# A planned start-up of an attention and mixer kernel: other load paces, phi's maxima on TensorE, another shape for the loads of one weight

## The chip, the cores and the metric

One core of one Trainium2 chip. The metric is the device time of one execution in microseconds (us).

## What is computed

`q`, `k`, `v` are (8 batches, 8 heads, 576 rows, 64) and `phi` (8, 8, 576, 32), all float32; the four mixer weights come as float64.

```python
a = softmax over s of phi                     # per (b, h, m)
k_m = einsum('bhsm,bhsd->bhmd', a, k);  v_m = the same of v
attn = softmax(q @ k_m.T / 8) @ v_m           # 32 memory slots
x = attn, heads side by side                  # (8, 576, 512)
u = x + (relu(x.T @ w_tok1) @ w_tok2).T       # mixes the 576 rows
out = u + relu(u @ w_ch1) @ w_ch2             # mixes the 512 channels, 1536 hidden
```

## The kernel before, in words

The work has two halves. The attention part runs per *quad*: four heads of one batch, so (b, Q) with Q = 0, 1 gives 16 quads. The channel part runs over nine *chunks* of 512 output rows, each in twelve blocks f of 128 hidden units: a first product (`mm_1`, L140, 12 matmuls of 512 columns), a relu that splits its result into a high (ScalarE, L113) and a low part (VectorE, L116), and a second product (`ch2`, `second`, L179, 12 matmuls). Every operand of a product is split in two parts, hence three matmuls for each.

The float64 weights are loaded as pairs of 32-bit words and turned into a high and a low part on the chip (`Piece`): `low_bits` (ScalarE, L615), `join` (VectorE, L620), `signs` (ScalarE, L626), `rebase` (VectorE, L629), `apply` (VectorE, L635), then for each weight in the piece `part_high` (ScalarE, L642) and `part_low` (GpSimd, L646). Piece f holds `w_ch1`'s columns and `w_ch2`'s rows of block f: the tiles `c1h`/`c1l` and, in the profile, `c`. `PartC1.load` (L717) loads `w_ch1`'s 512 rows x 128 columns of float64 by four DMAs; each fills 32 partitions with four rows of 1 KB. `PartC2.load` (L743) is one DMA of 128 rows.

A quad does: load phi, k, v, q; the maximum of phi over the rows; subtract, exponentiate (L312, L322); the product with k and v (`kvp`, L930 in `EarlyQuad`, L345 in `Quad`); scaling; the scores (L975, L413), a softmax over 32 slots; transposes (L987, L952); the token products `Ap` (L519), `Rp` (L538) and four `u` (L559). For batch 0 the maximum across partitions is taken by TensorE: `phi_turn` transposes (L911), `phi_diag` reduces and spreads it on a diagonal (L915), `phi_spread` multiplies it by ones (L921). For batch 1 it is `partition_all_reduce` on GpSimd (L1062), for quad (2,0) likewise, and there its sum too (L1291). `EarlyQuad` gets the sum as a column of ones in the kv product.

The order of the start is not written by hand. Steps for batches 0 and 1, the conversion of all weights, the 23 products of chunk 0, and the first loads of quad (2,0) are `Step`s with an engine, a cost in us, predecessors and `Room`s (buffers that it takes or uses). `plan` (a list scheduler) picks the engine that can begin first, among its steps that can begin within PATIENCE the one with the longest way to the end, and so writes one order for each engine, which then runs in that order. A load's landing is estimated from kb: 270 units per us, where a weight piece counts its words (1024) and 1.5 us of latency is assumed; a GpSimd reduction counts as 8.0 us. Twelve raw buffers ("homes") hold the pieces: `wide` (five buffers shared with activations, two of them for raw pieces, one after piece 7), `st0`, `st1`, and `kv`. Filler matmuls (L877) stand in long planned gaps of TensorE before the first product. From block 12 on a hand-written loop over chunks runs, with attention steps at set places.

SyncE (SP) issues all loads in the planned order; a DMA whose buffer is still in use holds those behind it.

Of the kernel before, what the change touches and what calls it, by code (L numbers as in the profile page):

```python
# [19 lines left out]
P = 128  # L20
# [7 lines left out]
def kernel(  # L28
# [559 lines left out]
    class Piece:  # L588
# [11 lines left out]
        def load(s, room):  # L600
            tag = room.tag
            name = f"raw{s.parts[0].name}"
            if tag == "wide":
                at = wide(I32, name).rearrange("p a (n t) -> p (a n) t", t=2)
            else:
                at = sb.tile([P, 1024, 2], I32, tag=tag, name=name, bufs=1)
# [77 lines left out]
    class PartW2:  # L684
        words, loads = NT * HALF, 2
# [20 lines left out]
    class PartC1:  # L706
        words, loads = DM, 4
# [20 lines left out]
    class PartC2:  # L728
        words, loads = DM, 1
# [39 lines left out]
    class Step:  # L769


        def __init__(s, eng, us, fn, after, take, use, kb):
            s.eng, s.us, s.fn, s.after, s.take, s.kb = eng, us, fn, list(after), take, kb
# [7 lines left out]
    def step(eng, us, fn, *after, take=(), use=(), kb=0):  # L781
        steps.append(Step(eng, us, fn, after, list(take), list(use), kb))
        return steps[-1]
# [3 lines left out]
    def plan():  # L787
# [6 lines left out]
        order, seen = [], set()  # L794
        for z in steps:
            stack = [(z, iter(then[z]))] if z not in seen else []
            seen.add(z)
            while stack:
                y, it = stack[-1]
                for x in it:  # L800
                    if x not in seen:
                        seen.add(x)
                        stack.append((x, iter(then[x])))
                        break
                else:
                    stack.pop()
                    order.append(y)
        for z in order:
            lag = 2.0 + z.kb / 270 if z.eng == "SP" else LAG.get(z.eng, 0.07)
            way[z] = z.us + lag + max((way[x] for x in then[z]), default=0)  # L810
        free, taken, landed = {}, {}, 0.0
        left, done = set(steps), []

        def when(z):
            t = free.get(z.eng, 0.0)
            for y in z.after:
                if y.ready is None:
                    return None
                t = max(t, y.end if y.eng == z.eng != "SP" else y.ready if z.eng != "SP" or y.eng != "SP" else y.end)
# [20 lines left out]
        while left:  # L840
            times = {}
            for z in left:
                t = when(z)
                if t is not None:
                    times[z] = t
            first = {}
            for z, t in times.items():
# [4 lines left out]
                key=lambda z: (way[z], -steps.index(z)),  # L852
# [11 lines left out]
            done.append(z)  # L864
        return sorted(done, key=lambda z: z.begin)

    PATIENCE = 0.3
    LATE = 3
    now = [None]

    def ps_tile(room, shape, name):

        pool = pch if room.tag == "ch" else pat if room.tag == "at" else pacc
        t = pool.tile(shape, F32, tag=room.tag, name=name, bufs=dict(room.tags)[room.tag])
# [9 lines left out]
    class EarlyQuad(Quad):  # L884
# [153 lines left out]
        def loads(s):  # L1038
# [3 lines left out]
            s.l_phi = step("SP", 1.25, s.load_phi, take=[s.phi], kb=288)  # L1042
            s.l_kv = step("SP", 2.5 * len(s.kvs), s.load_kv, take=s.kvs, kb=1152)
            s.l_q = step("SP", 3.1, s.load_q, take=[s.qroom], kb=576)

        def plan(s, w1, w2, taken, chunk):


            s.up = {}

# [7 lines left out]
            if s.b:  # L1058

                def reduce():  # L1060
                    s.r = sb.tile([P, 4 * M], F32, tag="pr", name="prr" + s.n, bufs=3)
                    nc.gpsimd.partition_all_reduce(s.r, s.m, P, RED.max)  # L1062

                z = step("POOL", 8.0, reduce, z, take=[pr2], use=[pr])
                where = pr2
            else:
                bk, where, col = s.bank(), s.bank(), s.of("ps", 2)
                z = step("PE", 0.3, lambda: s.phi_turn(bk), z, take=[bk], use=[pr])
                z = step("DVE", 0.6, s.phi_diag, z, take=[col, pr2], use=[bk])
                z = step("PE", 0.6, lambda: s.phi_spread(where), z, take=[where], use=[pr2])  # L1070

            z = step("DVE", 0.83, s.phi_sub, z, use=[s.phi, where])
            z = step("ACT", 0.76, s.phi_only_exp, z, use=[s.phi])

# [81 lines left out]

    def piece(tags, *parts, after=(), more=()):

        p = Piece(*parts)
        us = 0.12 + 1.08e-3 * p.words  # L1160
# [3 lines left out]
            take=[raw, *more], kb=p.words,  # L1164
        )
        loads.append(z)
        z = step("ACT", us - 0.05, p.low_bits, z, use=[raw])
        z = step("DVE", us, p.join, z, use=[raw])
        y = step("ACT", us, p.signs, z, use=[raw])
        z = step("DVE", 0.15 + 0.54e-3 * p.words, p.rebase, z, use=[raw])  # L1170
        z = step("DVE", us, p.apply, y, z, use=[raw])
        out = []
        for x, part in enumerate(parts):
            us = 0.12 + 1.08e-3 * part.words
            h = step("ACT", us, lambda x=x: p.part_high(x), z, take=part.rooms(), use=[raw])
            pool = True
            l = step(
                "POOL" if pool else "DVE", 0.15 + 2.3e-3 * part.words if pool else us,
                lambda x=x: p.part_low(x, nc.gpsimd if pool else nc.vector), h, use=[raw],
# [7 lines left out]
    WIDE, KV = [("wide", 5)], [("kv", 1)]  # L1187
# [7 lines left out]
    homes = [WIDE, ST[0], ST[1], WIDE, WIDE, ST[0], ST[1], WIDE, WIDE, KV, WIDE, KV]  # L1195
# [42 lines left out]
    def first_product(f):  # L1238
        bk, hh, hl = Room(("ch", 2)), Room(("hh", 2)), Room(("hl", 2))

        def mm():
# [4 lines left out]
            2.76, mm, *w_c[f][0], *(a.lows + c.lows if f == 0 else ()), take=[bk], use=room0  # L1246
# [31 lines left out]
    ends = [  # L1278
        step("SP", 2.5, second.load_kv, *w_c[NF - 1][1], take=[kv2], kb=1152),
        step("SP", 9.0, second.load_q, quads[1, 1].x_A, take=[q2], kb=576),  # L1280
        took2,
    ]
    for op, name in ((RED.max, "prr"), (RED.add, "psr")):
        pr, pr2 = Room(("pr", 3)), Room(("pr", 3))

        def red(op=op):
            second.m = second._red(ALU.max if op == RED.max else ALU.add)

        def reduce(op=op, name=name):
            second.r = sb.tile([P, 4 * M], F32, tag="pr", name=name + second.n, bufs=3)  # L1290
            nc.gpsimd.partition_all_reduce(second.r, second.m, P, op)  # L1291

        z = step("DVE", 1.3, red, z, take=[pr], use=[phi2])
        z = step("POOL", 8.0, reduce, z, take=[pr2], use=[pr])
        if op == RED.max:
            z = step("DVE", 0.83, second.phi_sub, z, use=[phi2, pr2])
            z = step("ACT", 0.76, second.phi_only_exp, z, use=[phi2])
    o0 = Room(("wide", 5))
    for x in range(NKK):
        ends.append(  # L1300
            step(
                "POOL", 1.4, lambda x=x: chunks[0].residual([x]), *a.lows, *c.lows, products[-4],
                use=[*room0] + ([o0] if x else []), take=[] if x else [o0],
            )
        )
# [131 lines left out]
```

## Time and profile before

| | us |
|---|---|
| median of 3 runs | 848.76 (848.4 to 850.31) |
| the profiled execution | 849.89 |
| its span, first to last instruction | 848.1 |
| TensorE matmul busy | 805.1 (95%) |
| VectorE busy | 411.7 (49%) |
| ScalarE busy | 221.6 (26%) |
| GpSimd busy | 139.6 (16%) |

The mean granted TensorE clock is 0.978 of full. PE is TensorE's matmuls, PEld its weight loads, DVE VectorE, ACT ScalarE, POOL GpSimd, SPq the DMA queue of SyncE. Spans on POOL are rough for library operations: the record of a reduction is a mark within the time that it holds the engine. In a timeline "x4" merges four instructions, and the bracket gives the idle time before the row and what ended it.

### The profile page before, as it was taken

Reading aid. Unit: us, or ns where it says so; the run is one execution under the profiler, and the core shown is the slowest. Engines: PE = TensorE matmul, PEld = TensorE weight load, DVE = VectorE, ACT = ScalarE, POOL = GpSimd, SP = SyncE. Lnnn points to the kernel's source line nnn. Section 1 sums busy time; section 2 is a strip of 40 time slices with the busy share of each in tenths; the row PEclk is TensorE's granted clock in tenths of the full one; section 3 lists DMA queues with packets and bytes.
Section 4 is the critical chain, followed back from the end, with each engine's and each line's share of the span. In section 5 each row is a group of like instructions: output and inputs, shape, how many; then the busy total and the mean of one; then the engine's idle time right before and its main releaser. Section 6 shows DMA issues by size and latency. Waiting matters only on the chain.

```text
span 848.1 us, 11688 instructions
## 1 busy us (share of the span) xinstructions
PE 805.1 (95%) x4648; PEld 660.3 (78%) x4648; DVE 411.7 (49%) x696; ACT 221.6 (26%) x430; POOL 139.6 (16%) x138
## 2 busy tenths in 40 slices
PE   6778994999999999999999999999999999999997
PEld 4576673887788888878787878787878788888886
DVE  5775875346445544464437443744364522213115
ACT  4475644322121222212222222222222221111110
POOL 1134431601013101210121001200030030202000
PEclk9888997899999999999999999999999999999999
DMA  8995830433321331223122422242214000200202
GB/s 214 234 217 124 182 82 18 105 99 70 79 42 57 61 87 19 60 60 70 42 43 65 83 57 43 56 93 56 43 56 78 1 1 1 50 1 0 50 1 49
DMA packets 133877, 58.29 MB, mean 69 GB/s; under 512 B 81984, under 2 KB 131136, under 8 KB 133824
## 3 DMA queue, kind: packets, MB, share of 16 engines
q1 hardware_dynamic: 132736, 57.04, 30.1%
q10 hardware_dynamic: 1088, 0.52, 0.3%
q8 instruction: 36, 0.59, 0.3%
q14 instruction: 17, 0.14, 0.0%
HBM read 48.10 MB, written 9.44 MB: 68 GB/s over the span
## 4 chain that ended last, share of the span: by engine, by line
PE 81%; DMA 6%; SPq 4%; POOL 3%; issue 2%; DVE 2%; ACT 1%; POOLq 0%; ACTq 0%; DVEq 0%
PE cp L140 33%; PE acc L179 31%; PE u L559 8%; DMA rawc<-in_moe_w_ch_dram 6%; PE Ap L519 2%; PE kvp L345 2%; PE sp L413 2%; SPq L898 1%; POOL c1l L646 1%; PE Rp L538 1%; PE end L179 1%; POOL c L646 1%; SPq L717 1%; SPq L269 1%; POOL o L191 1%
## 5 line engine op out<-in xcount | busy, mean ns | idle before, releaser
L179 PE MATMUL acc<-hh,c 128*128 128x512 f32 x832 | 281.0, 399 | 0.0
L116 DVE SCALAR_TENSOR_TENSOR hl<-cp,hh 128x512 fp32r<-128x512 f32 x104 | 71.8, 690 | 247.3 <-ACT hh L113 247.3
L179 PEld LDWEIGHTS acc<-hh,c 128*128 128x128 f32 x832 | 156.8, 188 | 36.6 <-issue 0.9
L140 PE MATMUL cp<-uh,c1l 128*128 128x512 f32 x432 | 172.2, 399 | 13.5 <-POOL c1l L646 13.5
L140 PE MATMUL cp<-uh,c1h 128*128 128x512 f32 x432 | 173.7, 402 | 0.0
L140 PE MATMUL cp<-ul,c1h 128*128 128x512 f32 x432 | 170.4, 394 | 0.0
L179 PE MATMUL acc<-hl,c 128*128 128x512 f32 x416 | 164.3, 395 | 0.0
L113 ACT ACTIVATE hh<-cp 128x512 fp32r<-128x512 f32 x104 | 62.2, 598 | 237.0 <-PE cp L140 237.0
L140 PEld LDWEIGHTS cp<-uh,c1l 128*128 128x128 f32 x432 | 82.2, 190 | 33.4 <-POOL c1l L646 15.4
L140 PEld LDWEIGHTS cp<-uh,c1h 128*128 128x128 f32 x432 | 82.2, 190 | 23.3 <-issue 7.6
L140 PEld LDWEIGHTS cp<-ul,c1h 128*128 128x128 f32 x432 | 82.1, 190 | 16.5
L179 PEld LDWEIGHTS acc<-hl,c 128*128 128x128 f32 x416 | 78.5, 189 | 15.9
L191 POOL TENSOR_TENSOR o<-uh,ul 128x512 f32<-128x512 f32 x36 | 47.3, 1341 | 114.6 <-issue 69.8
L464 POOL TENSOR_TENSOR al<-aT,ah 128x576 fp32r<-128x576 f32 x16 | 23.9, 1493 | 250.7 <-ACT ah L460 229.6
L572 ACT COPY rest<-u 128x288 f32<-128x288 f32 (+8 forms) x48 | 15.4, 321 | 92.5 <-PE u L559 87.5
L298 DVE TENSOR_REDUCE pr<-phi 128x128 f32<-128x640 f32 x28 | 36.4, 1304 | 5.7 <-DMA phi<-in_phi_dram 4.6
L559 PE MATMUL u<-w2h,Rh 128*128 128x288 f32 x128 | 38.7, 303 | 0.0
L559 PE MATMUL u<-w2h,Rl 128*128 128x288 f32 x128 | 38.7, 302 | 0.0
L559 PE MATMUL u<-w2l,Rh 128*128 128x288 f32 x128 | 38.7, 302 | 0.0
L580 DVE TENSOR_TENSOR ul<-u,uh 128x288 fp32r<-128x288 f32 (+8 forms) x48 | 16.8, 356 | 35.1 <-ACT uh L574 35.1
L331 POOL PARTITION_ALL_REDUCE psr<-pr x11 | 11.9, 1078 | 111.8 <-DVE pr L298 111.8
L116 DVE SCALAR_TENSOR_TENSOR Rl<-Rp,Rh 128x512 fp32r<-128x512 f32 x16 | 11.1, 691 | 37.1 <-ACT Rh L113 37.0
(154 smaller groups left out, 994.6 us busy)
## 6 DMA issues: line engine op xcount, KB each, us to landing
out_dram<-rows SPq DMA_DIRECT2D x32, 256.0 KB, 4.6
kv<-in_k_dram SPq DMA_DIRECT2D x15, 512.0 KB, 4.2
kv<-in_v_dram SPq DMA_DIRECT2D x15, 512.0 KB, 5.4
q<-in_q_dram SPq DMA_DIRECT2D x96, 72.0 KB, 2.5
rawc<-in_moe_w_ch_dram SPq DMA_DIRECT2D x48, 128.0 KB, 6.3
rawc<-in_moe_w_ch_dram SPq DMA_DIRECT2D x12, 512.0 KB, 7.3
phi<-in_phi_dram SPq DMA_DIRECT2D x16, 256.0 KB, 3.1
q<-in_q_dram SPq DMA_DIRECT2D x16, 128.0 KB, 4.3
```

The source lines that it names most:

```text
L113: nc.scalar.activation(out=h, in_=ps, func=AF.Relu)
L116: nc.vector.scalar_tensor_tensor(out=l, in0=ps, scalar=0.0, in1=f32(h), op0=ALU.max, op1=ALU.subtract)
L140: nc.tensor.matmul(ps, l[:, a, w], r[:, a], start=a == 0 and x == 0, stop=a == NKK - 1 and x == 2,)
L179: nc.tensor.matmul(ps, l_[f // 2][:, f % 2, a * P : (a + 1) * P], r[:, w], start=f == start and x == 0, stop=f == end - 1 and x == 2,)
L191: nc.gpsimd.tensor_tensor(out=s.o[:, a], in0=f32(s.uh[:, a]), in1=f32(s.ul[:, a]), op=ALU.add)
L298: nc.vector.tensor_reduce(out=m.rearrange("p (i m) -> p i m", i=4), in_=s.pt.rearrange("p i j m -> p i m j"), axis=AX.X, op=op,)
L345: nc.tensor.matmul(s.kvp[32 * i : 32 * i + 32, : 2 * D], s.pt[:n, i, j, :], s.kv[i][:n, :, j, :], start=j == 0, stop=j == NC - 1,)
L413: nc.tensor.matmul(ps[64 * p : 64 * p + 64, :HALF], s.kb[:, 64 * p : 64 * p + 64], s.qT[:, p, hf * HALF : (hf + 1) * HALF], start=True, st ...
L464: nc.gpsimd.tensor_tensor(out=s.al, in0=s.aT, in1=f32(s.ah), op=ALU.subtract)
L519: nc.tensor.matmul(ps[:, :TT], a, w, start=x == 0, stop=x == len(mm) - 1)
L559: nc.tensor.matmul(ps[:, :HALF], a, r, start=x == 0, stop=x == len(mm) - 1)
L646: eng.tensor_tensor(out=part.l, in0=part.pick(f32(part.raw[..., 0])), in1=f32(part.h), op=ALU.subtract)
```

## The change

- The loads of `w_ch1`: still four DMAs for a piece, each of which now fills all 128 partitions with one row of 1 KB, read as 4 groups x 32 rows.
- Batch 1's and quad (2,0)'s maximum of phi goes by the three steps on TensorE and VectorE that batch 0 has (`plan_phi`); quad (2,0) becomes a `ThirdBatchQuad`, whose sum comes from the column of ones.
- The planner: a load's time is given as `move` in us (c1 2.8, c2 2.4, kv 4.5, q 2.6, phi 1.2), with 2.4 us of latency and a MARGIN; costs of the conversion steps are adjusted; ranks get a HASTE of 20 us for steps that hold a shared PSUM bank (`at`, `ch`) and a random factor of up to 1.2 with a set seed; PATIENCE 0.3 becomes 0.1, LATE 3 becomes 2. LATE says how many products later than its set place an attention step of batch 1 may come.
- Buffers: pieces 0 and 1 are loaded into the tiles of `c2` of blocks 6 and 4, piece 9 into `st1`, 11 into `wide`; none into `kv`.
- The load of k and v for quad (2,0) no longer waits for the last piece; the four residual adds of chunk 0 run one after another.

```diff
-            for x in range(4):
-                nc.sync.dma_start(
-                    out=raw[32 * x : 32 * x + 32].rearrange("p (a n) t -> p a (n t)", a=NKK),
-                    in_=place(w_ch1[x * P : (x + 1) * P, s.w]).rearrange("(a c) n -> c a n", c=32),
-                )
+            src = place(w_ch1[:, s.w]).rearrange("(x a c) n -> a x c n", x=4, c=32)
+            dst = raw.rearrange("p (a n) t -> a p (n t)", a=NKK)
+            for a in range(NKK):
+                nc.sync.dma_start(out=dst[a], in_=src[a])
...
-            if s.f < NF - 4 or s.f % 2:
+            if s.f < 4 or s.f % 2:
                 return []
-            s.held.append(Room((f"st{(s.f - NF + 4) // 2}", 1)))
+            s.held.append(Room((f"st{(s.f - NF + 4) // 2}" if s.f >= NF - 4 else f"c2{s.f}", 1)))
...
+            s.held = [room for room in (*take, *use) if room.tags[0][0] in ("at", "ch")]
...
+            lag = 2.4 + z.move if z.eng == "SP" else LAG.get(z.eng, 0.07)
             way[z] = z.us + lag + max((way[x] for x in then[z]), default=0)
+        rank = {}
+        for n, z in enumerate(steps):
+            haste = HASTE if z.held and not z.take else 0
+            rank[z] = (way[z] * (1 + NOISE * vary.random()) + haste, -n)
...
-                landed = max(landed, z.begin + 1.5) + z.kb / 270
-                z.ready = max(landed + 0.4, z.end + 1.0)
+                landed = max(landed, z.begin + 2.4) + z.move
+                z.ready = max(landed + MARGIN, z.end + 1.0)
...
-    PATIENCE = 0.3
-    LATE = 3
+    PATIENCE = 0.1
+    LATE = 2
+    MARGIN = 0.3
+    HASTE = 20.0
+    NOISE, SEED = 0.2, 192
...
-            if s.b:
-                def reduce():
-                    s.r = sb.tile([P, 4 * M], F32, tag="pr", name="prr" + s.n, bufs=3)
-                    nc.gpsimd.partition_all_reduce(s.r, s.m, P, RED.max)
-                z = step("POOL", 8.0, reduce, z, take=[pr2], use=[pr])
-                where = pr2
-            else:
-                bk, where, col = s.bank(), s.bank(), s.of("ps", 2)
...
+            bk, where, col = s.bank(), s.bank(), s.of("ps", 2)
+            s.x_p1 = z = step("PE", 0.35, lambda: s.phi_turn(bk), z, take=[bk], use=[pr])
+            z = step("DVE", 0.6, s.phi_diag, z, take=[col, pr2], use=[bk])
+            s.x_p2 = z = step("PE", 0.65, lambda: s.phi_spread(where), z, take=[where], use=[pr2])
...
+    class ThirdBatchQuad(EarlyQuad):
+        load_q, q_turn = Quad.load_q, Quad.q_turn
+        def step_kv(s):
+            s.mm_kv(Room(BANKS[0]))
+            return s.spread_kv
...
-    homes = [WIDE, ST[0], ST[1], WIDE, WIDE, ST[0], ST[1], WIDE, WIDE, KV, WIDE, KV]
+    homes = [[("c26", 1)], [("c24", 1)], ST[0], ST[1], WIDE, WIDE, ST[0], ST[1], WIDE, ST[1], WIDE, WIDE]
...
-            [(qd.x_q0, h0), (qd.x_q1, h0 + 1), (qd.x_kv, h0), ...
+            [(qd.x_p1, h0 - 3), (qd.x_p2, h0 - 2), (qd.x_q0, h0), (qd.x_q1, h0 + 1), (qd.x_kv, h0), ...
...
-    second = Quad(2, 0)
-    phi2, kv2, q2 = Room(("phi", 2)), Room(("kv", 1)), Room(("big", 1))
-    z = step("SP", 1.25, second.load_phi, take=[phi2], kb=288)
-    ends = [
-        step("SP", 2.5, second.load_kv, *w_c[NF - 1][1], take=[kv2], kb=1152),
...
-    for op, name in ((RED.max, "prr"), (RED.add, "psr")):
...
+    second = ThirdBatchQuad(2, 0)
+    second.phi, kv2, q2 = Room(("phi", 2)), Room(("kv", 1)), Room(("big", 1))
+    second.l_phi = step("SP", 1.25, second.load_phi, take=[second.phi], move=1.2)
+    z = second.plan_phi()
+    step("SP", 2.5, second.load_kv, take=[kv2], move=4.5)
```

## Rows read from the trace of the kernel before

**Rows 1.** Busy time of each engine in three stretches (from:to in us, the stretch's length, then per engine us and count of instructions), with TensorE's granted clock, the DMA engines' busy share and GB/s.

```profile
0.00:63.00 63.00, 44.34 (x385) 37.42 (x385) 42.53 (x75) 33.45 (x61) 15.04 (x29) 0.89 0.95 222
63.00:178.00 115.00, 97.42 (x594) 78.12 (x595) 69.04 (x93) 52.00 (x86) 44.93 (x33) 0.91 0.44 104
178.00:842.00 664.00, 663.29 (x3672) 544.79 (x3670) 299.28 (x527) 136.14 (x284) 79.60 (x76) 1.00 0.22 48
```

**Rows 2.** Waits in 0 to 178 us: who waited for whom, us in total, times, longest.

```profile
PE cp L140 <- POOL c1l L646: 13.5, 4, 8.7
...
ACT rawc L615 <- DMA rawc<-in_moe_w_ch_dram: 11.2, 7, 2.6
```

**Rows 3.** Timeline of POOL, and when the reductions of quad (2,0) are set up on its queue (the row with min/median/max ns, first and last start).

```profile
44.59 2.89 POOL L646 TENSOR_TENSOR w2l<-raww,w2h 128x576 fp32r<-128x576 f32 x2 [3.62 <-DMA rawc<-in_moe_w_ch_dram]
...
65.52 1.18 POOL L1062 PARTITION_ALL_REDUCE prr<-pr  x1 [6.18 <-DMA rawc<-in_moe_w_ch_dram]
73.47 1.54 POOL L646 TENSOR_TENSOR c1l<-rawc,c1h 128x512 fp32r<-128x512 f32 x1 [6.76 <-ACT c L642]
...
89.90 2.01 POOL L1062 PARTITION_ALL_REDUCE prr<-pr  x1 [7.33 <-issue]
98.89 1.72 POOL L646 TENSOR_TENSOR c1l<-rawc,c1h 128x512 fp32r<-128x512 f32 x1 [6.98 <-ACT rawc L615]
...
122.00 0.72 POOL L1291 PARTITION_ALL_REDUCE prr<-pr  x1 [5.91 <-DMA rawc<-in_moe_w_ch_dram]
131.23 1.31 POOL L646 TENSOR_TENSOR c<-rawc,c 128x512 fp32r<-128x512 f32 x1 [8.51 <-ACT hh L113]
138.76 1.09 POOL L1291 PARTITION_ALL_REDUCE psr<-pr  x1 [6.22 <-PE u L559]
146.75 1.28 POOL L646 TENSOR_TENSOR c1l<-rawc,c1h 128x512 fp32r<-128x512 f32 x1 [6.90 <-issue]
...
165.06 1.30 POOL L646 TENSOR_TENSOR c1l<-rawc,c1h 128x512 fp32r<-128x512 f32 x1
...
L1291 POOLq MODIFY_POOL_CONFIG  x4: 3/8/12, 116.3 to 132.8; - x4
```

**Rows 4.** Timeline of ACT: the high parts that the low part at 146.75 reads.

```profile
134.29 0.65 ACT L642 CAST c1h<-rawc 128x512 fp32r<-128x512 f32 x1 [2.16 <-DVE rawc L635]
```

**Rows 5.** Timeline of PE (start, duration) at the four waits for `c1l`: behind the first some of the slow matmuls, and two at full pace.

```profile
75.06 0.80 PE L140 MATMUL cp<-uh,c1l 128*128 128x512 f32 x1 [2.82 <-POOL c1l L646]
75.65 0.63 PE L140 MATMUL cp<-uh,c1h 128*128 128x512 f32 x1
76.08 0.63 PE L140 MATMUL cp<-ul,c1h 128*128 128x512 f32 x1
...
82.75 0.40 PE L179 MATMUL acc<-hh,c 128*128 128x512 f32 x1
82.98 0.39 PE L140 MATMUL cp<-uh,c1h 128*128 128x512 f32 x1
...
100.66 0.50 PE L140 MATMUL cp<-uh,c1l 128*128 128x512 f32 x1 [1.35 <-POOL c1l L646]
...
148.08 0.80 PE L140 MATMUL cp<-uh,c1l 128*128 128x512 f32 x1 [8.73 <-POOL c1l L646]
...
166.41 0.51 PE L140 MATMUL cp<-uh,c1l 128*128 128x512 f32 x1 [0.61 <-POOL c1l L646]
```

**Rows 6.** Timelines of PE and ACT around the wait for `Ah`.

```profile
48.63 0.58 PE L538 MATMUL Rp<-vh,Ah 128*128 128x256 f32 x1 [4.55 <-ACT Ah L1008]
...
50.11 0.44 PE L559 MATMUL u<-ah,vh 128*128 128x288 f32 x1
...
47.21 1.10 ACT L615 ACTIVATE rawc<-rawc 128x1024 int32<-128x1024 uint32 x1 [2.07 <-DMA rawc<-in_moe_w_ch_dram]
48.22 0.36 ACT L1008 CAST Ah<-Ap 128x256 fp32r<-128x256 f32 x1
```

**Rows 7.** Two stretches with the columns of rows 1: loads of `w_tok1` and of k and v, 128 partitions each; loads of four pieces.

```profile
7.00:10.00 3.00, 2.46 (x10) 2.19 (x11) 2.18 (x6) 0.28 (x1) 0.00 (x0) 1.00 1.05 369
28.00:48.00 20.00, 12.60 (x81) 9.56 (x80) 15.41 (x29) 11.98 (x22) 6.22 (x6) 0.93 1.09 230
```

**Rows 8.** SP's queue: the issues of pieces 8 to 11 (L717 is c1, L743 c2), and its waits in 0 to 178 us.

```profile
85.20 3.94 SPq L717 DMA_DIRECT2D rawc<-in_moe_w_ch_dram  x4
...
118.22 2.58 SPq L717 DMA_DIRECT2D rawc<-in_moe_w_ch_dram  x4
...
149.31 1.74 SPq L717 DMA_DIRECT2D rawc<-in_moe_w_ch_dram  x4
...
SPq L717 <- POOL c L646: 27.8, 4, 15.0
SPq L717 <- PE kvp L930: 17.0, 1, 17.0
```

**Rows 9.** Batch 0's two maxima on TensorE: min/median/max ns, first and last start.

```profile
L911 PE MATMUL mt<-ident,pr x2: 474/475/476, 5.8 to 7.0; 128*128 128x128 f32 x2
L921 PE MATMUL mb<-dg,ones x4: 421/422/550, 8.0 to 8.8; 128*128 128x128 f32 x4
```

**Rows 10.** Busy time of PE and PEld in a stretch with one kv product: with the column of ones (L930), and without (L345).

```profile
116.00:119.00 3.00, 1.69 (x80) 1.59 (x80) 1.00 0.02 5
183.00:186.00 3.00, 1.43 (x40) 0.97 (x40) 1.00 0.05 3
```

More of the change, by code (lines that the diff above doesn't have):

```diff
@@ L1 @@
 import math
+import random
 from contextlib import ExitStack
@@ L605, in load @@
             else:
-                at = sb.tile([P, 1024, 2], I32, tag=tag, name=name, bufs=1)
+                pool = wp if tag[0] == "c" else sb
+                at = pool.tile([P, 1024, 2], I32, tag=tag, name=name, bufs=1)
             n = 0
@@ L684 @@
     class PartW2:
-        words, loads = NT * HALF, 2
+        words, loads, move = NT * HALF, 2, 2.7
         def __init__(s, hf):
@@ L706 @@
     class PartC1:
-        words, loads = DM, 4
+        words, loads, move = DM, 4, 2.8
         def __init__(s, f):
@@ L728 @@
     class PartC2:
-        words, loads = DM, 1
+        words, loads, move = DM, 1, 2.4
         held = []
@@ L769, with __init__ @@
     class Step:
-        def __init__(s, eng, us, fn, after, take, use, kb):
-            s.eng, s.us, s.fn, s.after, s.take, s.kb = eng, us, fn, list(after), take, kb
+        def __init__(s, eng, us, fn, after, take, use, move):
+            s.eng, s.us, s.fn, s.after, s.take, s.move = eng, us, fn, list(after), take, move
             s.begin = s.end = s.ready = None
             s.fill = 0
+            s.held = [room for room in (*take, *use) if room.tags[0][0] in ("at", "ch")]
             for room in (*take, *use):
@@ L779, with step, plan @@
     steps = []
-    def step(eng, us, fn, *after, take=(), use=(), kb=0):
-        steps.append(Step(eng, us, fn, after, list(take), list(use), kb))
+    def step(eng, us, fn, *after, take=(), use=(), move=0.0):
+        steps.append(Step(eng, us, fn, after, list(take), list(use), move))
         return steps[-1]
     LAG = {"PE": 0.25, "POOL": 0.15, "SP": 0.0}
-    def plan():
+    def plan(seed):
+        vary = random.Random(seed)
         then = {z: [] for z in steps}
@@ L792, in plan @@
                 then[y].append(z)
-        way = {}
[L794 to L804, printed above, removed]
-                else:
[L806 to L809, printed above, removed]
-            way[z] = z.us + lag + max((way[x] for x in then[z]), default=0)
+        needs = {z: len(z.after) for z in steps}
+        sorted_, free_ = [], [z for z in steps if not z.after]
+        while free_:
+            z = free_.pop()
+            sorted_.append(z)
+            for x in then[z]:
+                needs[x] -= 1
+                if not needs[x]:
+                    free_.append(x)
+        way = {}
+        for z in reversed(sorted_):
+            lag = 2.4 + z.move if z.eng == "SP" else LAG.get(z.eng, 0.07)
+            way[z] = z.us + lag + max((way[x] for x in then[z]), default=0)
+        rank = {}
+        for n, z in enumerate(steps):
+            haste = HASTE if z.held and not z.take else 0
+            rank[z] = (way[z] * (1 + NOISE * vary.random()) + haste, -n)
+        needs = {z: len(z.after) for z in steps}
         free, taken, landed = {}, {}, 0.0
-        left, done = set(steps), []
+        left, done = [z for z in steps if not z.after], []
         def when(z):
@@ L816, in when @@
             for y in z.after:
-                if y.ready is None:
-                    return None
-                t = max(t, y.end if y.eng == z.eng != "SP" else y.ready if z.eng != "SP" or y.eng != "SP" else y.end)
+                t = max(t, y.end if y.eng == z.eng else y.ready)
             more = {}
@@ L840, in plan @@
         while left:
[L841 to L845, printed above, removed]
+            times = {z: t for z in left if (t := when(z)) is not None}
             first = {}
@@ L851, in plan @@
                 (z for z, t in times.items() if z.eng == eng and t <= first[eng] + PATIENCE),
-                key=lambda z: (way[z], -steps.index(z)),
+                key=rank.get,
             )
@@ L864, in plan @@
             done.append(z)
+            for x in then[z]:
+                needs[x] -= 1
+                if not needs[x]:
+                    left.append(x)
         return sorted(done, key=lambda z: z.begin)
-    PATIENCE = 0.3
-    LATE = 3
+    PATIENCE = 0.1
[3 more added lines that the diff above has]
+    NOISE, SEED = 0.2, 192
     now = [None]
     def ps_tile(room, shape, name):
-        pool = pch if room.tag == "ch" else pat if room.tag == "at" else pacc
-        t = pool.tile(shape, F32, tag=room.tag, name=name, bufs=dict(room.tags)[room.tag])
+        tag = room.tag or room.tags[0][0]
+        pool = pch if tag == "ch" else pat if tag == "at" else pacc
+        t = pool.tile(shape, F32, tag=tag, name=name, bufs=dict(room.tags)[tag])
         flat = t if len(shape) == 2 else t.rearrange("p a n -> p (a n)")
@@ L1041, in loads, with plan_phi @@
             s.qroom = s.of(*(("rest", 1), ("big", 1), ("wide", 5))[(s.b, s.Q) != (0, 1) and 1 + (s.b and s.Q)])
[L1042 to L1049, printed above, removed]
+            s.l_phi = step("SP", 1.25, s.load_phi, take=[s.phi], move=1.2)
+            s.l_kv = step("SP", 2.5 * len(s.kvs), s.load_kv, take=s.kvs, move=3.5 + len(s.kvs))
+            s.l_q = step("SP", 3.1, s.load_q, take=[s.qroom], move=2.6)
+        def plan_phi(s):
             pr, pr2 = s.of("pr", 3), s.of("pr", 3)
@@ L1057, in plan @@
             z = step("DVE", 1.27, red, s.l_phi, take=[pr], use=[s.phi])
-            if s.b:
-                def reduce():
-                    s.r = sb.tile([P, 4 * M], F32, tag="pr", name="prr" + s.n, bufs=3)
-                    nc.gpsimd.partition_all_reduce(s.r, s.m, P, RED.max)
-                z = step("POOL", 8.0, reduce, z, take=[pr2], use=[pr])
-                where = pr2
-            else:
-                bk, where, col = s.bank(), s.bank(), s.of("ps", 2)
-                z = step("PE", 0.3, lambda: s.phi_turn(bk), z, take=[bk], use=[pr])
-                z = step("DVE", 0.6, s.phi_diag, z, take=[col, pr2], use=[bk])
-                z = step("PE", 0.6, lambda: s.phi_spread(where), z, take=[where], use=[pr2])
+            bk, where, col = s.bank(), s.bank(), s.of("ps", 2)
+            s.x_p1 = z = step("PE", 0.35, lambda: s.phi_turn(bk), z, take=[bk], use=[pr])
+            z = step("DVE", 0.6, s.phi_diag, z, take=[col, pr2], use=[bk])
+            s.x_p2 = z = step("PE", 0.65, lambda: s.phi_spread(where), z, take=[where], use=[pr2])
             z = step("DVE", 0.83, s.phi_sub, z, use=[s.phi, where])
             z = step("ACT", 0.76, s.phi_only_exp, z, use=[s.phi])
+            return z
+        def plan(s, w1, w2, taken, chunk):
+            s.up = {}
+            z = s.plan_phi()
             kvp, ms, T, vb = s.bank(), s.of("ms"), s.of("pr", 3), s.of("vb")
@@ L1163, in piece @@
             "SP", 0.62 * sum(part.loads for part in parts), lambda: p.load(raw), *after,
-            take=[raw, *more], kb=p.words,
+            take=[raw, *more], move=sum(part.move for part in parts),
         )
         loads.append(z)
-        z = step("ACT", us - 0.05, p.low_bits, z, use=[raw])
-        z = step("DVE", us, p.join, z, use=[raw])
+        z = step("ACT", us, p.low_bits, z, use=[raw])
+        z = step("DVE", vs, p.join, z, use=[raw])
         y = step("ACT", us, p.signs, z, use=[raw])
-        z = step("DVE", 0.15 + 0.54e-3 * p.words, p.rebase, z, use=[raw])
-        z = step("DVE", us, p.apply, y, z, use=[raw])
+        z = step("DVE", 0.15 + 0.6e-3 * p.words, p.rebase, z, use=[raw])
+        z = step("DVE", vs, p.apply, y, z, use=[raw])
         out = []
@@ L1175, in piece @@
             h = step("ACT", us, lambda x=x: p.part_high(x), z, take=part.rooms(), use=[raw])
-            pool = True
             l = step(
-                "POOL" if pool else "DVE", 0.15 + 2.3e-3 * part.words if pool else us,
-                lambda x=x: p.part_low(x, nc.gpsimd if pool else nc.vector), h, use=[raw],
+                "POOL", 0.15 + 2.3e-3 * part.words, lambda x=x: p.part_low(x), h, use=[raw]
             )
@@ L1186 @@
     ST = [("st0", 1)], [("st1", 1)]
-    WIDE, KV = [("wide", 5)], [("kv", 1)]
+    WIDE = [("wide", 5)]
     quads = {(b, Q): EarlyQuad(b, Q) for b in range(2) for Q in range(2)}
@@ L1245, in first_product @@
         z = product(
-            2.76, mm, *w_c[f][0], *(a.lows + c.lows if f == 0 else ()), take=[bk], use=room0
+            2.8, mm, *w_c[f][0], *(a.lows + c.lows if f == 0 else ()), take=[bk], use=room0
         )
@@ L1253, in second_product @@
         product(
-            2.76, lambda: chunks[0].ch2(f), *w_c[f][1], *ready[f][:2],
+            2.8, lambda: chunks[0].ch2(f), *w_c[f][1], *ready[f][:2],
             take=accs if f == 0 else (), use=ready[f][2:],
@@ L1273 @@
                 products[h + LATE].after.append(z)
-    second = Quad(2, 0)
-    phi2, kv2, q2 = Room(("phi", 2)), Room(("kv", 1)), Room(("big", 1))
-    z = step("SP", 1.25, second.load_phi, take=[phi2], kb=288)
-    ends = [
-        step("SP", 2.5, second.load_kv, *w_c[NF - 1][1], take=[kv2], kb=1152),
-        step("SP", 9.0, second.load_q, quads[1, 1].x_A, take=[q2], kb=576),
-        took2,
-    ]
-    for op, name in ((RED.max, "prr"), (RED.add, "psr")):
[L1284 to L1297, printed above, removed]
@@ L1298 @@
-    o0 = Room(("wide", 5))
-    for x in range(NKK):
[L1300 to L1304, printed above, removed]
+    second = ThirdBatchQuad(2, 0)
+    second.phi, kv2, q2 = Room(("phi", 2)), Room(("kv", 1)), Room(("big", 1))
+    second.l_phi = step("SP", 1.25, second.load_phi, take=[second.phi], move=1.2)
+    z = second.plan_phi()
@@ L1305 @@
+    step("SP", 2.5, second.load_kv, take=[kv2], move=4.5)
+    step("SP", 9.0, second.load_q, quads[1, 1].x_A, take=[q2], move=3.0)
+    o0, y = Room(("wide", 5)), products[-4]
+    for x in range(NKK):
+        y = step(
+            "POOL", 1.4, lambda x=x: chunks[0].residual([x]), *a.lows, *c.lows, y,
+            use=[*room0] + ([o0] if x else []), take=[] if x else [o0],
         )
     step(
-        "END", 0, None, z, *ends, products[-1], *ready[NF - 1][:2],
+        "END", 0, None, z, took2, products[-1], *ready[NF - 1][:2],
@@ L1308 @@
         *(y for Q in range(2) for y in quads[1, Q].lows + quads[1, Q].highs),
-        use=[*PartC2.held, *room1, rest_room, phi2, pr2, kv2, q2, o0, *accs, *ready[NF - 1][2:], *room0],
+        use=[*PartC2.held, *room1, rest_room, second.phi, kv2, q2, o0, *accs, *ready[NF - 1][2:], *room0],
     )
-    order = plan()
+    order = plan(SEED)
     idle = 0.0
```

10 lines of the change are left out of this document (5 added, 5 removed).

## The prediction, before the result was known

> **What bounds the kernel now.** I first read the busy time by stretches [rows 1]. From 178 to 842 us TensorE (PE) is busy 663.29 of 664 us at the full clock: that steady part can only get shorter by less work on PE, and the change takes none away there. The first 178 us are the head that the planner orders. In 0 to 63 us PE is busy 44.34 us, part of it with filler products (L877), while the DMA engines are busy (share 0.95): batch 0 waits for loads and for the conversion of weights. In 63 to 178 us, where the 23 planned products run, PE is busy 97.42 of 115 us and idle 17.6, at a mean granted clock of 0.91, and the DMA engines are used at 0.44 only. So the head is bound by waits in chains, neither by bandwidth nor by PE.
>
> The table of waits [rows 2] names them: 13.5 of the 17.6 us are four waits of the first channel product (L140) for `c1l`, which GpSimd (POOL) makes at L646. The POOL timeline [rows 3] shows why: it holds four `partition_all_reduce`, marked at 65.52, 89.90, 122.00 and 138.76. Each has 5.9 to 7.3 us of idle before it and 6.8 to 8.5 us after it; the last is set up at 132.8, and the next low part begins at 146.75. So one holds POOL for some 14 us, where the planner counts 8.0. Three of the four waits (2.82, 1.35 and 8.73 us [rows 5], together 12.9) end with the first `c1l` after a reduction; 0.61 us belongs to piece 11, loaded late. `c1h` for the longest wait was written by 134.94 [rows 4], 11.8 us before its `c1l` began: POOL alone held PE. Behind such a wait the next matmuls run at the lower clock: 0.43 us apart against 0.23.
>
> A fifth wait of 4.55 us is of another kind [rows 6]: PE waits for `Ah`, whose copy stands on ScalarE (ACT) behind the first conversion step (L615) of a weight that had not landed. ACT sat 2.07 us for the landing. The old planner moves 1,049 KB of a piece in 1024/270 = 3.8 us; in the stretch of these loads the rate was 230 GB/s [rows 7], 4.6 us each. Orders written for 3.8 us put ACT work behind loads that come later.
>
> Last, the loads of the tail [rows 8]: piece 9 goes out at 118.22 after 17.0 us for quad (1,1)'s kv product, and piece 11 at 149.31, up to 15.0 us for POOL's low part of piece 9, since both use the `kv` buffer. `c1l` of piece 11 comes at 166.4 [rows 3].
>
> **The change, part by part.** The sum is made against the profiled execution (849.89 us, span 848.1), 1.1 us over the median of the runs.
>
> *Phi's maxima.* Four POOL reductions leave the head (two of batch 1, two of quad (2,0)); its sum too comes out of the product with a column of ones. A low part takes 1.3 us, so the 24 of them hold POOL for 31 us in all. I take 13.5 us off, bounds 13.5 and 5 (if late landings take the reductions' place). Of the lower clock I take off the 14 slow matmuls after the 2.82 us wait and the 10 after the 8.73 us one: 24 x 0.20 = 4.8 us, bounds 0 and 4.8.
> On PE come three times a turn (0.47 us, L911) and a spread (2 records of 0.42, some 0.6 together, L921), as batch 0 has them [rows 9]: 3 x 1.1 = 3.3 us; and quad (2,0)'s kv product with its 40 further matmuls takes 1.69 instead of 1.43 us [rows 10], 0.26. Together +3.5, bounds +0.3 (all in gaps of PE) and +8, because each chain also holds both `at` banks over a reduction and a scaling on VectorE (DVE). DVE is busy 69 of the 115 us: some 2 us more fit.
>
> *The planner.* Its paces are now 2.8 + 2.4 = 5.2 us for a piece, above the 4.6 measured, so ACT should no longer stand ahead of a landing. The `Ah` wait is worth at most 4.55 us, at least 0. Of it u can use less: it also needs `w2l`, which POOL ends at 47.5 [rows 3], while u began at 50.1 [rows 6]. I take 2.5.
>
> *Buffers.* Pieces 0 and 1 go where c2 of 6 and 4 will stand, 9 into `st1`, 11 into `wide`; the kv buffer leaves the tail. A piece with no reduction in its way needs 17 us from issue to its last low (piece 11, 149.31 to 166.4). The planner has one late room for pieces 8, 10 and 11: issued at 85.2 as now and one after the other, they are ready at 102, 119 and 136. PE would want piece 11 at about 166.4 - 15 = 151. So I cost the rooms at nothing; the cover is 15 us. Without this part piece 11 would go on at 166.4, and the first term would be lost again there.
>
> *Moved steps.* load_phi issues two DMAs and a POOL memset of 0.2 us, load_kv four DMAs, load_q of (2,0) eight; they pass pieces on SP at 0.3 to 0.6 us each. SP stands still for up to 17 us in this stretch [rows 8], so nothing, at most 5 us if q's eight stand in front of a piece. The four residual adds keep their 1.3 us each.
>
> *c1's load.* Four DMAs of 131 KB as before, 1 KB a row as before. I count no gain and no loss. A floor: the k and v loads, 1 KB rows onto 128 partitions, stand in a stretch that moved 369 GB/s [rows 7], which would make c1 0.9 us shorter a piece, in a place with cover. The ceiling is the first rival.
>
> *What is late next.* The other waits of the 17.6 us (4.1) stay, and batch 1's chain over DVE and ACT gets a shorter stretch to hide in: +2, bounds 0 and +8.
>
> Sum: -13.5 - 4.8 + 3.5 - 2.5 + 2 = -15.3, so 834.6 for an execution like the profiled one, 833.5 for the median.
>
> **The rivals.** *c1 on four DMA engines.* All loads of before have 32, 64 or 128 as their outermost count. The new source's outermost count is 4 (x of "x c n"), the target's 128. If four engines do the work, the engines' 369/16 = 23 GB/s give 524 KB in 5.7 us instead of 2.3: 3.4 us more a piece, and 8.0 against the planner's 5.2. Then ACT stands ahead of landings again, four pieces in a row by up to 11 us. Part is covered (15 us in the tail, gaps of the DMA engines): I take 8 us back, 841.5, within 834 to 848. For it: every other load of this kernel keeps a large count outermost. Against it: no DMA in the trace has so small a one, so no row shows what it costs.
> The Trainium skill, DMA: Bandwidth & Descriptors, section Rules for kernel authors, says it outright: the slowest dimension of either side sets how many engines share a DMA, and one of size c under 16 confines it to at most c. No run here shows it so far. By that rule alone the sum is the rival's 841.5, by the rows alone 833.5.
>
> *Slower.* The late room serialises pieces 8, 10 and 11. If slow c1 loads make piece 8 ready 14 us later (four pieces x 3.4), at 116, and a piece in that room takes 28 us instead of 17, its conversions queued in order behind others, piece 11 is ready at 116 + 56 = 172 instead of 166.4, and the end is at some 855. It decides from the point where the two take over 25 us each. For it: piece 9, issued at 118.22, had its low parts only at 149.3, 31 us. Against: two reductions stood in its way, and they go.
>
> *More.* All 17.6 us, the 4.55 and the slow matmuls vanish and c1 gets faster: -13.5 - 4.1 - 4.8 - 4.6 + 3.5 = -23.5, with 2 us more of u at the lower clock: 823.
>
> *No change.* The new order brings a new wait on DVE or a bank for each one lost: 848.
>
> **How the numbers follow.** Forecast 833.5 (0.38), four engines 841.5 (0.33), slower 855 (0.13), more 823 (0.10), none 848 (0.06). Each case has some 7 us about it. The range 820 to 848 takes in all but the slower one and small tails; the forecast's own range is 826 to 841. A measurement of this kernel tells 0.2%, 1.7 us, from no change: faster 0.81, same 0.06, slower 0.13.
>
> **What would show it.** Right: no PARTITION_ALL_REDUCE before 178 us, the `c1l` waits of PE under 3 us, the steady part beginning near 162 instead of 177.7, about 670 us after that as before. The `Ah` copy not behind an L615 that waits. Four engines: c1 DMAs whose last one lands over 5 us after the first while GB/s falls under 130 in stretches of c1 alone, and `rawc` L615 waits for DMA well over the 11.2 us of before. Wrong: TensorE again short of `c1l`, now after late landings, or DVE over 90% busy from 60 us on.

## The result: slower by 0.9%

The changed kernel takes 857.46 us (median; 854.71 to 857.77) against 849.38 us for the kernel before in the same session: ratio 1.0088, 95% interval 1.0063 to 1.0113. The forecast was 833.5, range 820 to 848. The profiled execution took 857.39 us, its span 855.6. Medians below leave out one run of E4 (1141 us) and one of E11 (1316 us), in which TensorE's granted clock was 0.65 and 0.56.

Busy time by stretches of the changed kernel, the columns of [rows 1]:

```profile
0.00:63.00 63.00, 47.24 (x392) 39.87 (x393) 49.16 (x78) 32.93 (x61) 16.46 (x30) 0.86 0.68 180
63.00:178.00 115.00, 90.47 (x552) 70.72 (x552) 68.74 (x92) 50.74 (x82) 39.31 (x27) 0.91 0.51 127
178.00:842.00 664.00, 663.40 (x3695) 545.03 (x3694) 295.12 (x515) 137.60 (x288) 81.66 (x79) 1.00 0.22 47
```

In 63 to 178 us PE is now idle 24.5 us where it was 17.6. In the first 63 us, where loads were the resource in use, the DMA share fell from 0.95 to 0.68 and the rate from 222 to 180 GB/s: less is moved, with engines standing idle. The stretch of the first pieces and the queue's packets (page part 3: packets, MB, share), which answer to [rows 7]:

```profile
28.00:48.00 20.00, 14.44 (x78) 11.85 (x79) 18.63 (x29) 11.79 (x22) 6.11 (x5) 0.73 0.55 167
...
q1 hardware_dynamic: 132160, 57.03, 28.6%
```

The same line of the kernel before:

```profile
q1 hardware_dynamic: 132736, 57.04, 30.1%
```

230 GB/s at a share of 1.09 became 167 at 0.55. The queue has 576 packets fewer with the same bytes: 12 for each of the 48 DMAs of c1. The waits of the head, answering to [rows 2]:

```profile
PE np L993 <- DVE aT L457: 6.9, 3, 3.4
PE acc L180 <- ACT hh L114: 6.5, 1, 6.5
PE sp L981 <- ACT kb L950: 3.9, 2, 3.0
...
PE cp L141 <- POOL c1l L648: 0.9, 1, 0.9
...
ACT rawc L617 <- DMA rawc<-in_moe_w_ch_dram: 36.9, 11, 7.0
```

The 13.5 us for `c1l` have shrunk to 0.9. In their place ScalarE waits 36.9 us, in 11 places, for pieces to land, where it was 11.2. The longest PE wait shows the link; ACT and PE timelines, as in [rows 6]:

```profile
70.72 1.14 ACT L617 ACTIVATE rawc<-rawc 128x1024 int32<-128x1024 uint32 x1 [6.85 <-DMA rawc<-in_moe_w_ch_dram]
71.73 0.66 ACT L644 CAST c1h<-rawc 128x512 fp32r<-128x512 f32 x1
72.28 0.62 ACT L114 ACTIVATE hh<-cp 128x512 fp32r<-128x512 f32 x1
...
72.95 0.80 PE L180 MATMUL acc<-hh,c 128*128 128x512 f32 x1 [6.53 <-ACT hh L114]
...
185.21 0.40 PE L141 MATMUL cp<-uh,c1h 128*128 128x512 f32 x1
```

The relu of a finished product (`hh`) stands on ACT behind the first conversion step of a piece that has not landed. The last row is the first matmul of the hand-written loop: 185.2 instead of 177.7, the whole 7.5 us by which the span grew.

### The profile page after: what moved, and what is told of

Read it like the earlier page. It is cut to its first block, busy times and chain, and to the rows that moved or that the text cites. A ratio compares the mean times of both kernels' runs of the same rounds, so it can differ in the third digit from the quotient of the medians.

```text
span 855.6 us, 11760 instructions
## 1 busy us (share of the span) xinstructions
PE 808.6 (95%) x4697; PEld 662.9 (77%) x4697; DVE 420.0 (49%) x699; ACT 221.3 (26%) x430; POOL 137.4 (16%) x134
## 4 chain that ended last, share of the span: by engine, by line
PE 79%; SPq 13%; DMA 3%; issue 3%; POOL 1%; DVE 1%; ACT 0%; POOLq 0%; ACTq 0%
PE cp L141 32%; PE acc L180 31%; PE u L560 7%; SPq L721 5%; PE Ap L520 2%; DMA rawc<-in_moe_w_ch_dram 2%; SPq L744 2%; SPq L904 2%; PE kvp L346 2%; PE sp L414 2%; PE Rp L539 1%; SPq L270 1%; PE end L180 1%; DMA phi<-in_phi_dram 1%; SPq L266 1%
## 5 line engine op out<-in xcount | busy, mean ns | idle before, releaser
L180 PE MATMUL acc<-hh,c 128*128 128x512 f32 x832 | 284.8, 403 | 6.5 <-ACT hh L114 6.5
L180 PEld LDWEIGHTS acc<-hh,c 128*128 128x128 f32 x832 | 159.2, 191 | 43.1 <-ACT hh L114 6.7
L141 PE MATMUL cp<-uh,c1l 128*128 128x512 f32 x432 | 170.1, 394 | 0.9 <-POOL c1l L648 0.9
L180 PE MATMUL acc<-hl,c 128*128 128x512 f32 x416 | 166.3, 400 | 0.0
L573 ACT COPY rest<-u 128x288 f32<-128x288 f32 (+8 forms) x48 | 15.3, 320 | 95.4 <-PE u L560 90.4
L622 DVE SCALAR_TENSOR_TENSOR rawc<-rawc 128x1024 int32<-128x1024 int32 x12 | 16.5, 1373 | 31.0 <-ACT rawc L617 31.0
L520 PE MATMUL Ap<-w1h,nat 128*128 128x256 f32 x144 | 28.4, 291 | 1.5 <-DVE nat L1006 1.5
```

Source lines behind the costliest of these rows:

```text
L141: nc.tensor.matmul(ps, l[:, a, w], r[:, a], start=a == 0 and x == 0, stop=a == NKK - 1 and x == 2,)
L180: nc.tensor.matmul(ps, l_[f // 2][:, f % 2, a * P : (a + 1) * P], r[:, w], start=f == start and x == 0, stop=f == end - 1 and x == 2,)
L520: nc.tensor.matmul(ps[:, :TT], a, w, start=x == 0, stop=x == len(mm) - 1)
```

## The experiments

Theory *Engines*: c1's new loads run on four of the 16 DMA engines, and that is the loss. Rival *Order*: the new order and the maxima lose by themselves. The kernel before was measured again with each set of runs (849.7 us with E1, E2 and E4; 850.2 with E5, E6, E8 and E9; 848.6 with E7, E10 and E11), and ratios are against the one of the same set. The names of the other theories are those of the expectations printed below.

**E1: the changed kernel with c1's old loads.** The planned order is the same.

```diff
...
-            for a in range(NKK):
-                nc.sync.dma_start(out=dst[a], in_=src[a])
+            for x in range(4):
+                nc.sync.dma_start(out=raw[32 * x : 32 * x + 32]..., in_=place(w_ch1[x * P : (x + 1) * P, s.w])...)
```

> The changed kernel with c1 loaded as before (four DMAs of 32 partitions each); the planned order stays the same to the instruction, since the planner's paces are not touched. If the four-engine loads are the loss (theory Engines): a piece lands in some 4.7 us instead of 7 to 8, ScalarE's L617 waits for rawc fall from 36.9 us to under 12, the steady loop begins at 160 to 168 us instead of 185.2, time 832 to 842. If the new order or phi's maxima on TensorE lose by themselves (theory Order): waits such as np on DVE aT and acc on ACT hh stay, loop at 180 or later, time 850 or more.

832.19 us, ratio to before 0.9796 (0.9766 to 0.9827). Stretches, and the first rows on PE of three landmarks (`kvp` of batch 1's two quads, and the loop):

```profile
63.00:160.00 97.00, 89.45 (x577) 73.02 (x576) 71.32 (x95) 50.44 (x84) 39.01 (x28) 0.95 0.46 116
...
28.00:48.00 20.00, 13.38 (x76) 10.99 (x77) 18.54 (x32) 11.48 (x21) 6.11 (x5) 0.76 1.09 256
...
78.84 0.32 PE L937 MATMUL kvp<-kv,phi 128*32 128x128 f32 x4
...
108.53 0.32 PE L937 MATMUL kvp<-kv,phi 128*32 128x128 f32 x4
...
162.38 0.40 PE L141 MATMUL cp<-uh,c1h 128*128 128x512 f32 x1
```

The same landmarks in the changed kernel:

```profile
84.96 0.41 PE L936 MATMUL kvp<-kv,phi 128*32 128x128 f32 x5
...
120.79 0.32 PE L936 MATMUL kvp<-kv,phi 128*32 128x128 f32 x4
```

With c1 on the new loads the head is 6.1 us late at the first landmark, 12.3 at the second and 22.8 at the loop: every burst of pieces adds to it. With the old loads ACT has no wait for the landing of a piece among its recorded ones. So the loss lies in the new loads, and Order falls.

That four engines carry these loads can be read where c1 of the last piece moves alone, between its first packets and those of c2 (the columns of [rows 1]). The changed kernel:

```profile
157.50:159.00 1.50, 0.95 (x7) 0.91 (x8) 0.73 (x2) 0.97 (x2) 0.00 (x0) 1.00 0.26 90
```

E1:

```profile
138.20:139.60 1.40, 1.40 (x12) 1.33 (x10) 0.46 (x1) 0.50 (x2) 0.00 (x0) 1.00 0.85 248
```

A share of 0.26 is that of some four of the 16 engines, one of 0.85 that of nearly fourteen.

**E2: the kernel before with c1's new loads alone.** Same edit, other way round.

> The kernel before with the new shape of c1's loads alone. Engines: 3.4 us more a piece, on an order made for 3.8 us a piece; between 4 and 12 pieces of it on the path, 14 to 41 us: 863 to 890. Order: within 3 us of 849.

878.75 us, ratio 1.0342 (1.0318 to 1.0366), and again 576 packets fewer. Some of its waits:

```profile
PE cp L140 <- POOL c1l L646: 16.4, 3, 9.5
PE Rp L538 <- ACT Ah L1007: 10.0, 1, 10.0
...
ACT rawc L615 <- DMA rawc<-in_moe_w_ch_dram: 46.8, 10, 7.9
```

The new loads cost 29 us in the old order and 25.3 in the new one. The `Ah` wait of [rows 6] doubled to 10.0.

**E4: the planner is told the pace.**

```diff
-        words, loads, move = DM, 4, 2.8
+        words, loads, move = DM, 4, 5.7
```

> The changed kernel, c1 still on four engines, but the planner is told 5.7 us for c1's four DMAs instead of 2.8. Engines: the order now waits where the loads are late, so ScalarE stands ahead of fewer landings (L617 waits under 20 us); part of the loss comes back, 845 to 853; the loads themselves still cost. Order: no systematic change, 857 with some 5 us either way from another draw of the order.

851.49 us, ratio 1.0019 (1.0004 to 1.0034). No ACT wait for a piece's landing is left, yet the time is only 6.0 us shorter: 126 GB/s at a share of 0.49 in 63 to 178 us, nearly as in the changed kernel.

```profile
63.00:178.00 115.00, 96.34 (x575) 77.29 (x574) 66.28 (x98) 53.02 (x87) 34.68 (x27) 0.87 0.49 126
```

So most of the 25.3 us stays while the loads are slow, even with an order that knows their pace. Whether the 6 us come from the right pace is not shown: the other pace also draws another order, and a draw alone can be worth some 9 us (E7).

**E8, E9, E10: c2's load on four, eight and sixteen engines.** All three are E1 but for this load. In every one of them c2 fills 128 partitions with one row of 4 KB each; the source's outermost count changes, and with it which row of `w_ch2` lands on which partition, so the second product pairs hidden units wrongly, at the same work. They tell the number of engines from the shape on the partitions (*Partitions*) and from the order of the rows in memory (*Row order*).

```diff
-                in_=place(w_ch2[s.f * P : (s.f + 1) * P]),
+                in_=place(w_ch2[s.f * P : (s.f + 1) * P]).rearrange("(c g) n -> g c n", g=4),   # 8, 32
```

> E1 with c2's load read as 4 groups of 32 rows, row 4c+g to partition 32g+c: one DMA, 128 partitions, 4 KB a row as in E1, only the source's outermost count is 4; the rows of w_ch2 stand in another order, so the second product pairs hidden units wrongly. If the number of engines sets the price (Engines): 131 KB on each of four engines at some 25 GB/s, 5.1 us instead of 2.3 for c2, 2.8 us more a piece, 12 packets fewer for each of 12 DMAs, 846 to 858. If filling all partitions with one row each was what slowed c1 (theory Partitions): c2 always did that, 830 to 835.

> As the kernel with 4 groups, with 8 groups of 16 rows (the order of w_ch2's rows changed likewise). Engines: 65 KB on each of eight engines, 2.6 us instead of 2.3, 8 packets fewer for each of 12 DMAs, 831 to 839. Partitions: 830 to 835.

> Control for the kernels with 4 and 8 groups: c2's rows are read in another order again (32 groups of 4 rows, row 32c+g to partition 4g+c, hidden units paired wrongly), but the source's outermost count is 32. Engines: all 16 engines carry it, the packets are those of E1 (132736), 830 to 836. If the order of the rows in memory was what cost 14 us with 8 groups and part of the 34 us with 4 (theory Row order): 838 or more.

Measured 865.88, 846.05 and 830.98 us (E1 832.19). The queue's packets and the stretch of the first pieces, four groups:

```profile
q1 hardware_dynamic: 132592, 57.04, 28.8%
...
28.00:48.00 20.00, 13.57 (x71) 11.40 (x72) 14.55 (x25) 9.87 (x19) 6.02 (x4) 0.69 0.63 165
```

Eight groups:

```profile
q1 hardware_dynamic: 132640, 57.04, 31.3%
...
28.00:48.00 20.00, 14.53 (x79) 12.42 (x79) 15.30 (x25) 11.15 (x21) 7.30 (x5) 0.74 0.85 176
```

Thirty-two groups:

```profile
q1 hardware_dynamic: 132736, 57.04, 30.1%
...
28.00:48.00 20.00, 14.70 (x85) 12.51 (x86) 18.69 (x27) 12.39 (x21) 6.11 (x5) 0.74 1.10 251
```

Against the 132736 of E1, packets fall by 144 = 12 x 12, 96 = 12 x 8 and 0: the number of engines follows the outermost count. It shows in the share too where c2 of the last piece moves alone. Four groups, eight groups, and E1:

```profile
166.00:171.00 5.00, 5.00 (x32) 4.46 (x33) 1.03 (x3) 1.32 (x3) 0.00 (x0) 1.00 0.24 82
```

```profile
152.00:155.00 3.00, 3.00 (x20) 2.64 (x19) 0.67 (x2) 0.00 (x0) 0.00 (x0) 1.00 0.45 115
```

```profile
140.40:141.60 1.20, 0.94 (x7) 0.90 (x8) 0.43 (x2) 0.96 (x2) 0.00 (x0) 1.00 0.85 324
```

Time follows the count as well, +33.7, +13.9 and -1.2 us. Both prices are above what was expected (at most 26 and 7): a size that the expectations missed. Partitions and Row order fall; that another row order costs nothing is shown for 32 groups alone. With E1 and E2, Engines holds.

**E5: E1 with the maxima on GpSimd; E6: the kernel before with the maxima on TensorE alone.** Theory *Maxima* against *Paces*.

```diff
E5
+            if s.b:
...
+                z = step("POOL", 8.0, reduce, z, take=[pr2], use=[pr])
...
E6, on the kernel before: plan_phi, ThirdBatchQuad and the two due times of x_p1, x_p2 as in the change
```

> E1 (the changed kernel with c1's old loads) with the maxima of phi of batch 1 and of quad (2,0) back on GpSimd, counted at 8.0 us by the planner; the sum of (2,0) stays a column of ones. If the maxima are worth what the c1l waits of before suggest (theory Maxima), three reductions that hold POOL some 14 us each delay low parts again: PE waits for c1l of 5 us or more, 838 to 848. If right load paces alone make the gain (theory Paces): 830 to 835.

> The kernel before with phi's part of the change alone (maxima on TensorE for batch 1 and quad (2,0), its sum by the column of ones), old paces, old buffers, old c1 loads, the order planned anew by the old planner. Maxima: the three c1l waits behind reductions (12.9 us) go and little takes their place, 833 to 841. Paces: ScalarE still stands ahead of loads that land later than planned, and the kv buffer holds pieces 9 and 11: 843 to 850.

E5: 848.15 us, ratio 0.9971 (0.9947 to 0.9995), just past the upper end of the band of Maxima. E6: 840.50, ratio 0.9881 (0.9856 to 0.9905), at the upper end of its band. The maxima alone bring 9.7 us; put back on GpSimd in E1 they cost 16. The sign in E5 was not quite the expected one (5 us or more for `c1l`):

```profile
PE acc L180 <- POOL c L648: 7.3, 1, 7.3
PE cp L141 <- ACT c1h L644: 6.2, 1, 6.2
...
PE cp L141 <- POOL c1l L648: 2.8, 3, 2.0
```

The reductions again have 5.8 to 6.2 us of idle before their marks. PE waits 7.3 us for a low part of c2 behind the first of them. The 6.2 us hang on the third, marked at 116.81, through a buffer (timelines of POOL, SP and ACT):

```profile
126.53 1.29 POOL L648 TENSOR_TENSOR c1l<-rawc,c1h 128x512 fp32r<-128x512 f32 x1 [9.00 <-issue]
127.79 3.10 POOL L648 TENSOR_TENSOR c<-rawc,c 128x512 fp32r<-128x512 f32 x2
...
129.12 1.76 SPq L719 DMA_DIRECT2D rawc<-in_moe_w_ch_dram  x4
...
135.77 1.10 ACT L617 ACTIVATE rawc<-rawc 128x1024 int32<-128x1024 uint32 x1 [11.55 <-DMA rawc<-in_moe_w_ch_dram]
```

The next load goes out when POOL has read the piece before it, and ACT waits for it to land. In E6 no wait of PE for `c1l` is left; its stretch up to the loop, which begins at 168.83:

```profile
63.00:169.00 106.00, 94.06 (x602) 75.49 (x603) 74.33 (x99) 52.47 (x86) 44.07 (x29) 0.97 0.44 109
```

The parts of the change other than the maxima and c1's loads are worth 2 us at most without the maxima, with them 8.3 (832.19 against 840.5): neither theory alone makes the 17.5.

**E7 and E11: E1 without the random factor, and with seed 7.** Theory *Draw*: the gain is that of one lucky order.

```diff
-    NOISE, SEED = 0.2, 192
+    NOISE, SEED = 0.0, 192      # E7
+    NOISE, SEED = 0.2, 7        # E11
```

> E1 with the planner's random factor off (NOISE 0). If the gain of E1 comes from paces and maxima (Maxima and Paces together): 829 to 840. If it comes from the one drawn order with seed 192 (theory Draw): 842 to 855.

> E1 with seed 7 in place of 192. Maxima and Paces: 829 to 840, as without the random factor. Draw: anywhere between 835 and 855, above E1.

841.30 us (ratio 0.9913, 0.9883 to 0.9944) and 833.63 (0.9807, 0.9774 to 0.9840). Seed 7 is within 1.4 us of seed 192; the order without the factor is 9 us behind, between the bands of the two theories. E7's order returns values that are off (by a relative 0.07), for a reason that is not known, so its time is the weaker evidence. As far as it goes, a draw can move the time by some 9 us, and E4, E5 and E6, whose orders are planned anew, carry such an uncertainty: their 6, 16 and 9.7 us are rough sizes. E1 and E11 beat both kernels.

## Why the prediction was wrong

**The failing step** is *c1's load*: "Four DMAs of 131 KB as before, 1 KB a row as before. I count no gain and no loss." It cost +25.3 us (857.46 - 832.19, from two sessions; +29 in the old order). The forecast looked at bytes, rows and count of DMAs and not at the outermost count of the source, 4, which decides how many engines take part. The packets, the share of 0.26 and E8 to E10 show it. The Trainium skill, DMA: Bandwidth & Descriptors, section Rules for kernel authors, has this rule, and the section Why a DMA increments its semaphore by 16 and not by 1 says that each engine that takes part ends with a write of its own: the traces agree, 12 packets fewer for a DMA on four engines. The prediction had that rule as its first rival and gave it 0.33, since no row of before showed it. That weight was too low.

**The rival's price** was the second miss: 8 us, "part is covered". The price of a piece was about right. In the second burst of the changed kernel the conversions of pieces follow each other by 7.9, 7.9 and 9.1 us, each after a wait for the landing, where the rival had 8.0:

```profile
89.65 1.13 ACT L617 ACTIVATE rawc<-rawc 128x1024 int32<-128x1024 uint32 x1 [1.78 <-DMA rawc<-in_moe_w_ch_dram]
97.55 1.14 ACT L617 ACTIVATE rawc<-rawc 128x1024 int32<-128x1024 uint32 x1 [4.27 <-DMA rawc<-in_moe_w_ch_dram]
105.43 1.13 ACT L617 ACTIVATE rawc<-rawc 128x1024 int32<-128x1024 uint32 x1 [1.70 <-DMA rawc<-in_moe_w_ch_dram]
114.57 1.14 ACT L617 ACTIVATE rawc<-rawc 128x1024 int32<-128x1024 uint32 x1 [2.93 <-DMA rawc<-in_moe_w_ch_dram]
```

The cover was wrong. Twelve pieces at 3.4 us are 41; the rival let 8 of them through, and 25 to 29 came, adding up burst by burst (6.1, 12.3, 22.8 us at the landmarks). The gaps of the DMA queue that looked like cover in [rows 1] (share 0.44) were in good part waits of SP for buffers ([rows 8]). Loads also go out later in the changed kernel, the last piece at 155.0 us where E1 has 136.7; how much of that is buffers that come free later, and how much the longer issues on SP, is not separated. The rival *slower* named such a chain, with 172 us for piece 11's `c1l`; it came at 172.1, from a head that was late throughout; that two slow stays in one room did it is not shown. The range ended at 848 because this case was left out of it.

**The other terms** can be read from E1, which is the change without the failing step: 832.19 against the forecast's 833.5. That it comes so close is in part luck: the first term below came out smaller and the parts beside it larger than forecast, and another seed or none gives 833.6 or 841.3.
- *Maxima*, -13.5 and -4.8 with +3.5 of new work: the c1l waits are gone in E1 and 0.9 us in the changed kernel. E6 gives -9.7 for this part alone, against a net -14.8: right in mechanism, a third too large. With no wait for `c1l` left in E6, it is not piece 11 in the `kv` buffer that holds PE, as *Buffers* feared; PE is idle 11.9 us of 63 to 169 us by other waits (`Tp` behind ACT's `qT` the longest, 4.2), where before had 4.1 of these.
- *The planner*, -2.5 for `Ah`: E1 has no wait of PE for `Ah` and none of ACT for a landing. With the other parts beside the maxima it brings 8.3 (E1 against E6), more than was forecast. The paces do what was said of them when the loads keep them; at 5.2 us planned and some 8 real, ACT stood ahead of landings again.
- *What is late next*, +2: PE is idle 7.6 us of 97 in E1, by short waits on DVE of up to 2.4 us (`mt`, `acc`, `u`). That is 3.5 more than the 4.1 that were not for `c1l` before, and 7.8 more in E6: within the bounds of 0 and +8.
- *The steady part*, 670 us: 670.4 after, as before. Its beginning in E1, 162.4, is the predicted "near 162"; the sum, -15.3, is the shift from 177.7.

**The signs** that the prediction named for four engines came: L617 waits for `rawc` 36.9 us, "well over the 11.2". With c1 alone the rate was 90 GB/s, under the 130 that were named; the 167 GB/s of the first pieces' stretch hold c2's full-width loads too.

## What to carry to other kernels

Before costing a reshaped DMA at nothing, write down the outermost count of both access patterns: bytes, rows and number of DMAs can all stay while three quarters of the engines drop out. A transfer share below one in a planned start is no sure cover if loads wait for buffers that earlier loads free; price a slower load as if all of it came through, then argue some away. When an order is planned from paces, a load slower than its pace stalls the in-order engine on which its consumer stands ahead of other work (here ACT, 36.9 us).

## What the runs showed that was not expected

- Eight engines for c2 cost 13.9 us. Moving alone, c2 ran at 82 GB/s on four engines, 115 on eight and 324 on all: divided by their number, some 20, 14 and 20 GB/s an engine. So with eight the packets took longer too, and it was not only that engines stood idle. Why is open.
- An issue on SP took longer with the new c1 loads: median 998 ns for the 48 DMAs against 423 before (this and the next fence: count, min/median/max ns, first and last start; changed kernel, then before). Why is not shown; in E2 the median is 576 ns and the loss no smaller.

```profile
L721 SPq DMA_DIRECT2D rawc<-in_moe_w_ch_dram x48: 531/998/3507, 26.1 to 156.7; - x48
```

```profile
L717 SPq DMA_DIRECT2D rawc<-in_moe_w_ch_dram x48: 311/423/1243, 26.3 to 150.6; - x48
```
